# Attention stage of an RWKV and two-MLP kernel: new order of TensorE's work, six tiles in flight, and some work moved between VectorE, GpSimd and ScalarE

## The chip, the cores and the metric

The kernel runs on one core of one Trainium2 chip. The metric is the device time of one execution in microseconds (us). The core has five engines that run their own instruction queues in order: TensorE (PE in the profile; PEld is its weight load), VectorE (DVE), ScalarE (ACT), GpSimd (POOL) and SyncE (SP), which issues most transfers. They meet through semaphores.

## The reference

Three stages follow one another: an RWKV-like attention over 768 tokens of 4 sequences with 8 heads of 48, a mixture of 8 experts of which each token takes one, and a dense two-layer network.

```python
B, H, S, D = 4, 8, 768, 48
for t in range(S):                                   # attention
    cur = einsum('bhd,bhe->bhde', u[None] * k[:, :, t], v[:, :, t])
    y[:, :, t] = einsum('bhd,bhde->bhe', r[:, :, t], state + cur)
    state = w[None, :, :, None] * state + einsum('bhd,bhe->bhde', k[:, :, t], v[:, :, t])
x = y.transpose(0, 2, 1, 3).reshape(3072, 384)
logits = x @ w_gate                                  # (3072, 8)
e = argmax(logits, 1); gate = softmax(logits)[arange(3072), e]
x = gate[:, None] * (maximum(x @ w1[e], 0) @ w2[e])  # for each token its expert, 384 -> 1024 -> 384
h = x @ w_in                                         # 384 -> 2048
out = (h - tanh(h)) @ w_out                          # 2048 -> 384
```

## The kernel before

**Tiles.** The attention is cut into 6 chunks (`c`) of 128 tokens for each of the 4 sequences (`b`), which makes 24 tiles, `seq[n] = (n // 4, n % 4)`. One pass of the main loop, `for n in range(NN + 1)`, is called step n here. All of this is written in an order by hand (`tc.manual_schedule()`): each engine takes its instructions in the order in which the program issues them.

**One tile.** The token-by-token recurrence is done in matrix form. `load(n)` brings r, k, v by token (`n_b[n % NB]`) and r, k transposed (`t_b[n % NB]`). `scale` (line 312) multiplies the transposed r and k with tables of powers of the decay. `scores` (line 353) makes the 128 by 128 products of k and r for each head, in two PSUM banks, one for each half of the array's rows. `side_rk`, `side_rku`, `side_kh` (lines 317, 323, 332, GpSimd) make r*k, r*k*u and the scaled k; `diag_sum` (337, VectorE) sums r*k*u over a head, `diag` (344, ScalarE) puts the sum on the diagonal of a matrix `am` for each head. `mask` (359, VectorE) copies the scores of earlier keys from PSUM into `am`. `state` (370 to 377) adds the tile's k and v products to the running state `Sc[b]`: GpSimd multiplies the old state with the decay (`sw`, 376), VectorE adds the PSUM product (377). `state_copy` (385, ScalarE) puts the two 64-row halves of it into a block matrix `Sb[b]`. `outp` (393, 398) multiplies `Sb` with the scaled r over all 128 rows and `am` with v over 48 output columns, in turn for two pairs of heads, and ScalarE copies the result to `y` (403).

**Behind each chunk** of four tiles, spread over the next steps: `logits` and `logits2` (413 to 422, TensorE) and `gate` (428 to 449, VectorE: `m`, `sh`, `sc`, `mx`, `ssum`, `OH`, ...) choose an expert for every token; `rank_mm` (468 to 471, TensorE) and `rank_sel` (476 to 501) find its place in the expert's list: VectorE makes `pr`, the rank, `ge`, `hs`, `ohh`, `lo`; GpSimd makes from `ohh` the products `hv` (490) and a first `rh` (494), ScalarE or GpSimd the second `rh` (497, 499), VectorE `ol` (501); `idx_mm` (510, TensorE) adds up the list of token numbers. `xout` (524 to 533) transposes y back and writes it to DRAM. The gate runs in steps 6, 10, 14, 18, 22, the ranks one step later, the lists one step behind that.

**Weights.** Each float32 weight is split in two parts for TensorE's faster float32r form: `w_split` casts on ScalarE (`nc.scalar.copy`, line 84) and subtracts the cast from the original on an engine given as `eng` (line 85), in the attention stage VectorE by default, later mostly GpSimd. Steps 3 to 18 each do one quarter of a pair of weight blocks.

**The step before the change** issues, in this order: `load(n+3)`, on odd steps `w_load`; `diag_sum(n+1)`, `scale(n+1)`; `logits`; `outp(n-1)`, `state_copy(n-1)`; `xout`; `diag(n+1)`; `scores(n)`, `mask(n)`; `state(n)`; `side(n+2)`, `side_kh(n+2)`; `logits2`, `gate`; `rank_mm`, `rank_sel`; `idx_mm`; `w_split`. In step 1 GpSimd also makes the constants of the later stages (`consts`, `gate_cols`).

Behind the attention the experts' blocks and then the dense network follow, which the change doesn't touch.

Of the kernel before, what the change touches and what calls it, by code (L numbers as in the profile page):

```python
# [30 lines left out]
def rwkv_moe_moe_kernel(ctx: ExitStack, tc: tile.TileContext, rk_t, rkv, pk, u, wp1, wp2, out):  # L31
# [161 lines left out]
    NB = 5  # L193
# [8 lines left out]
    Sc = [ap_.tile([P, HP, D], F32, name=f"Sc{b}") for b in range(B)]  # L202
    Sb = [ap_.tile([P, HP, P], F32, name=f"Sb{b}") for b in range(B)]
# [3 lines left out]
    PRK = ap_.tile([P, 2, HP, P], F32, name="PRK")  # L207
# [5 lines left out]
    yh = [psy.tile([P, BANK], F32, tag=f"y{d}", name=f"yh{d}")[:, 0:HEAD] for d in range(KD)]  # L213
    Yp = [t.rearrange("p (j t) -> p j t", t=P) for t in yh[0:2]]
    Pb = yh[2]
    Pp = Pb[:, 0:HP * D].rearrange("p (j d) -> p j d", d=D)
# [52 lines left out]
    def tables():  # L269

        for t, base, n in ((pw, wsafe.unsqueeze(2), 16), (pq, pw[:, :, 16:17], 8)):
            nc.vector.memset(t[:, :, 0:1], 1.0)
            nc.vector.tensor_copy(out=t[:, :, 1:2], in_=base)
            m = 1
            while m < n:
                nc.vector.tensor_tensor(out=t[:, :, m + 1:2 * m + 1], in0=t[:, :, 1:m + 1],
                                        in1=bc(t[:, :, m:m + 1], [P, HP, m]), op=ALU.mult)
                m *= 2
        table(nc.gpsimd, PRK[:, 0], pq[:, :, 0:8], pw[:, :, 0:16])
# [3 lines left out]
        table(nc.vector, PRK[:, 1], ipq[:, :, 0:8], ipw[:, :, 1:17])  # L283
# [19 lines left out]
    def zero_states():  # L303
        for b in range(B):
            nc.scalar.mul(out=Sb[b], in_=ident.unsqueeze(1).to_broadcast([P, HP, P]), mul=0.0)
# [57 lines left out]
    def state(n):  # L363
        c, b = seq[n]
        if c == C - 1:
            return
        kh = st.pop(("kh", n))
        for j in range(HP):
            for q in range(2):
                nc.tensor.matmul(Pp[64 * q:64 * q + D, j, :], lhsT=kh[:, 2 * j + q, :],  # L370
                                 rhs=n_b[n % NB][:, 2, 2 * j + q, :], start=True, stop=True)
        if c == 0:
            nc.vector.tensor_copy(out=Sc[b], in_=Pp)
        else:
            sw = at2.tile([P, HP, D], F32, tag="sw", name="sw")
            nc.gpsimd.tensor_tensor(out=sw, in0=Sc[b], in1=bc(pq[:, :, 8:9], [P, HP, D]), op=ALU.mult)
            nc.vector.tensor_tensor(out=Sc[b], in0=sw, in1=Pp, op=ALU.add)
        st["S", b] = n

    def state_copy(n):  # L380
        c, b = seq[n]
        if c == C - 1:
            return
        for q in range(2):
            nc.scalar.copy(out=Sb[b][64 * q:64 * q + 64, :, 64 * q:64 * q + D], in_=Sc[b][64 * q:64 * q + 64, :, :])

    def outp(n):
        c, b = seq[n]
        am = st.pop(("am", n))
        for j0 in range(0, HP, 2):  # L390
            for j in (j0, j0 + 1):
                if c > 0:
                    nc.tensor.matmul(Yp[j % 2][:, j // 2, :], lhsT=Sb[b][:, j, :], rhs=t_b[n % NB][:, 0, j, :],
                                     start=True, stop=False)
            for j in (j0, j0 + 1):
                for q in range(2):
                    p0 = 64 * q
# [75 lines left out]
    def rank_sel(c):  # L473
# [16 lines left out]
        nc.gpsimd.tensor_tensor(out=hv.rearrange("p b (e q) -> p b e q", q=4),  # L490
# [3 lines left out]
        nc.gpsimd.tensor_tensor(out=rh[:, :, 0, :], in0=hv,  # L494
                                in1=bc(tileid[:, c * B:(c + 1) * B].unsqueeze(2), [P, B, E * 4]), op=ALU.mult)
        if c == C - 2:
            nc.gpsimd.tensor_scalar(out=rh[:, :, 1, :], in0=hv, scalar1=pid, scalar2=None, op0=ALU.mult)
        else:
            nc.scalar.activation(out=rh[:, :, 1, :], in_=hv, func=ACTF.Copy, scale=pid)
# [48 lines left out]
    xgh = [n_b[i][:, 0].rearrange("p h d -> p (h d)") for i in (4, 0)]  # L548
# [7 lines left out]
    def head_tiles():  # L556
        flat = [ap_.tile([P, 2 * HP * P], F32R, tag=f"t{i}", name=f"f{i}") for i in range(NB)]
        xth.extend(flat[i][:, 0:KD * HEAD].rearrange("p (k t) -> p k t", k=KD) for i in (4, 0))
        h2h.extend(flat[i][:, 0:2 * HEAD].rearrange("p (s t) -> p s t", s=2) for i in (1, 2, 3))
# [12 lines left out]
    xg0 = [n_b[i][:, 0].rearrange("p h d -> p (h d)") for i in (1, 2)]  # L572
# [36 lines left out]
    def by_token():  # L609

        with tc.tile_pool(name="slow", bufs=1) as sp:
# [3 lines left out]
            for b in range(B):  # L615
                nc.vector.memset(Sc[b], 0.0)
# [5 lines left out]
            for c in range(C):  # L622
                st["y", c] = yp.tile([P, HP, B, P], F32, tag="y", name="y")
                for b in range(B):
# [5 lines left out]
                    with tc.For_i(0, P, 1) as t:  # L630
                        nc.vector.tensor_copy(out=oh, in_=bc(ident[:, bass.ds(t, 1)], [P, 64]))
                        vb = ps1.tile([P, HP, P], F32, tag="X", name="vb", bufs=2)[:, :, 0:D]
                        for q in range(2):
                            nc.tensor.matmul(vb[64 * q:64 * q + 64], lhsT=oh,
                                             rhs=n_b[n % 2][:, 2].rearrange("p (j q) d -> p q j d", q=2)[:, q],
                                             start=True, stop=True)
                        nc.vector.tensor_tensor(out=kv, in0=vb, in1=bc(kT[:, :, bass.ds(t, 1)], [P, HP, D]), op=ALU.mult)
                        nc.vector.tensor_tensor(out=cur, in0=kv, in1=bc(ucol.unsqueeze(2), [P, HP, D]), op=ALU.mult)
                        nc.vector.tensor_add(out=cur, in0=cur, in1=Sc[b])
# [7 lines left out]
                        nc.vector.tensor_tensor(out=Sc[b], in0=Sc[b], in1=bc(wcol.unsqueeze(2), [P, HP, D]), op=ALU.mult)  # L647
                        nc.vector.tensor_add(out=Sc[b], in0=Sc[b], in1=kv)
# [12 lines left out]
    with tc.manual_schedule():  # L661
# [35 lines left out]
        for t in Yp + [Pp]:  # L697
            nc.vector.memset(t, 0.0)
# [3 lines left out]
        for n in range(NN + 1):  # L702
            if n + 3 < NN:
                load(n + 3)
            if n % 2 == 1 and n // 4 < PRE:
                w_load(n // 4, n // 2 % 2)
            if n + 1 < NN:
                diag_sum(n + 1)
                scale(n + 1)
            at_step(n, 2, logits)  # L710
            if 1 <= n <= NN:
                outp(n - 1)
                if n > 1:
                    state_copy(n - 1)
            for m in XOUT.get(n, (n - LAG,)):
                if m >= 0:
                    xout(m)
            if 0 < n < NN - 1:
                diag(n + 1)
            if n < NN:  # L720
# [5 lines left out]
                else:  # L726
                    if n == 1:
                        state(0)
                    state(n)
            if n == 1:  # L730
                state_copy(0)
            if n + 2 < NN:
                side(n + 2)
                if n == 0:
                    side_kh(0)
                    side_kh(1)
                side_kh(n + 2)
            at_step(n, 3, logits2)
            at_step(n, 3, gate)
            if n == H0 * B + 3:  # L740
                head_count()
            at_step(n, 4, rank_mm)
            at_step(n, 4, rank_sel)
            if n == H0 * B + 3:
                head_end()
            if n < NN:
                at_step(n, 5, idx_mm)
# [11 lines left out]
            if n >= 3 and (n - 3) // 4 < PRE:  # L759
                w_split((n - 3) // 4, (n - 3) % 4)  # L760
# [642 lines left out]
```

## Time and profile before

| | |
|---|---|
| median of 3 runs | 816.72 us (815.63 to 817.61) |
| the profiled execution | 815.03 us, of which the span of its instructions is 812.9 us |
| TensorE, VectorE, ScalarE, GpSimd busy over the span | 96%, 80%, 65%, 55% |
| mean granted clock of TensorE | 0.991 of full speed |
| scores of tile 0, 6, 22, 23 start at | 10.49, 44.22, 139.13, 144.60 us |

A row of the timeline reads: start (us), duration (us), engine, line of the kernel, operation, output <- inputs by the program's names, shapes, count, and in brackets the idle time of the engine just before and what ended it. Rows of the same kind that follow one another are merged with their count. A row of the groups by line has: line, engine, operation, names, shapes, count, then busy us and the mean ns of one, then the idle us before and what ended most of it. TensorE's rows overlap, since its instructions are pipelined: what a group costs is read from the start of the next. A GpSimd or VectorE row's duration can hold waiting.

### The profile page before, as it was taken

What the parts mean: (1) busy time and instruction counts of PE and PEld (TensorE: products, weight loads), DVE (VectorE), ACT (ScalarE), POOL (GpSimd) and SP (SyncE); (2) the same over time, 40 slices, a digit from 0 to 9 for tenths busy, and PEclk for the clock granted to TensorE, in tenths of its full rate; (3) what the DMA queues carried; (4) which work ended last, traced back from release to release, by engine and by line L of the source; (5) the groups of instructions that cost most, each with busy time, mean ns of one, the idle gap of its engine ahead of it and who ended that gap; (6) DMA issues with size and microseconds to landing.
All of it is one profiled execution on the core that took longest, in us unless ns stands there. A gap on an engine that the chain in (4) does not pass through costs nothing.

```text
span 812.9 us, 14403 instructions
## 1 busy us (share of the span) xinstructions
PE 780.9 (96%) x5052; PEld 699.3 (86%) x5052; DVE 648.6 (80%) x1127; ACT 526.0 (65%) x1135; POOL 450.7 (55%) x438
## 2 busy tenths in 40 slices
PE   7789999899999999999999999999999999999995
PEld 6567776699899999999989999999999999999895
DVE  7798988449888888995498888888888888888991
ACT  8778887426454545545587776776777677677770
POOL 7987885127676776775445544434345354343532
PEclk9999999999999999999999999999999999999998
DMA  8979864236689889995400000001000000000000
GB/s 220 268 205 260 219 200 135 89 92 188 199 223 267 268 207 276 321 240 160 136 1 0 1 10 30 2 0 40 1 1 30 10 1 20 21 1 10 30 1 39
DMA packets 34979, 89.88 MB, mean 111 GB/s; under 512 B 5690, under 2 KB 13022, under 8 KB 34896
## 3 DMA queue, kind: packets, MB, share of 16 engines
q1 hardware_dynamic: 30704, 78.87, 34.2%
q0 software_dynamic: 4192, 9.99, 4.1%
q8 instruction: 42, 0.69, 0.4%
q14 instruction: 41, 0.34, 0.2%
HBM read 73.10 MB, written 15.74 MB: 109 GB/s over the span
## 4 chain that ended last, share of the span: by engine, by line
PE 49%; DVE 2%; issue 1%; POOL 1%; ACT 0%; POOLq 0%; DVEq 0%; ACTq 0%
PE h L1239 24%; PE o L1287 22%; PE y L1013 2%; PE hps L988 1%; DVE t L1260 0%; DVE h L1257 0%; DVE h L1258 0%; DVE h L1256 0%; DVE t L1255 0%; POOL out_dram L1300 0%; POOL g L1276 0%; ACT g L1275 0%; POOLq L1398 0%; ACT z L1243 0%; ACT t L1245 0%
## 5 line engine op out<-in xcount | busy, mean ns | idle before, releaser
L1276 POOL TENSOR_TENSOR g<-t,g 128x512 fp32r<-128x512 f32 x93 | 120.4, 1295 | 176.3 <-ACT g L1275 122.6
L1239 PE MATMUL h<-xb,ring 128*128 128x512 f32 x864 | 215.9, 395 | 0.7 <-DVE t L1260 0.7
L1287 PE MATMUL o<-ring,g 128*128 128x384 f32 x1116 | 209.3, 336 | 0.0
L1287 PEld LDWEIGHTS o<-ring,g 128*128 128x128 f32 x1116 | 196.1, 188 | 8.1
L1239 PEld LDWEIGHTS h<-xb,ring 128*128 128x128 f32 x864 | 161.3, 188 | 31.9 <-DVE t L1260 1.1
L85 POOL TENSOR_TENSOR ring<-stg,ring 128x384 fp32r<-128x384 f32 x102 | 105.0, 1052 | 57.1 <-ACT ring L84 50.2
L1243 ACT ACTIVATE z<-h 128x512 f32<-128x512 f32 x96 | 57.5, 599 | 98.0 <-PE h L1239 97.9
L1013 PE MATMUL y<-h,ring 128*128 128x256 f32 (+7 forms) x576 | 113.9, 342 | 0.0
L988 PE MATMUL hps<-xt,ring 128*128 128x472 f32 (+6 forms) x504 | 106.1, 354 | 1.8 <-DVE xt L977 0.9
L1013 PEld LDWEIGHTS y<-h,ring 128*128 128x128 f32 x576 | 101.4, 188 | 3.2
L1255 DVE TENSOR_TENSOR t<-t,h 128x512 f32<-128x512 f32 x96 | 65.7, 684 | 41.8 <-ACT t L1245 41.3
L988 PEld LDWEIGHTS hps<-xt,ring 128*128 128x128 f32 x504 | 90.5, 188 | 6.0 <-DVE xt L977 1.6
L84 ACT CAST ring<-stg 128x384 fp32r<-128x384 f32 x152 | 70.8, 512 | 19.1 <-DMA stg<-in_wp_dram 18.6
L1260 DVE COPY_PREDICATED t<-mk,h 128x512 f32<-128x512 uint32 x96 | 72.1, 751 | 9.9
L1257 DVE SCALAR_TENSOR_TENSOR h<-s,h 128x512 f32<-128x512 f32 x96 | 66.9, 696 | 11.4 <-ACT g L1275 1.4
L991 ACT ACTIVATE h<-hps 128x256 fp32r<-128x256 f32 (+7 forms) x64 | 32.0, 501 | 58.2 <-PE hps L988 50.7
L1247 ACT ACTIVATE s<-z,gb 128x512 f32<-128x512 f32 x96 | 69.6, 725 | 0.0
L1258 DVE SCALAR_TENSOR_TENSOR h<-z,h 128x512 f32<-128x512 f32 x96 | 66.8, 696 | 3.3
L1249 ACT ACTIVATE mk<-z,gt 128x512 f32<-128x512 f32 x96 | 69.3, 722 | 0.0
L1256 DVE TENSOR_TENSOR h<-h,z 128x512 f32<-128x512 f32 x96 | 66.4, 692 | 0.0
L1275 ACT CAST g<-t 128x512 fp32r<-128x512 f32 x93 | 57.6, 619 | 7.9 <-DVE t L1260 5.7
L344 ACT ACTIVATE am<-ident,dt 128x128 f32<-128x128 f32 x192 | 58.6, 390 | 4.4 <-DVE dt L337 4.2
(233 smaller groups left out, 1112.9 us busy)
## 6 DMA issues: line engine op xcount, KB each, us to landing
stg<-in_wp_dram SPq DMA_DIRECT2D x64, 384.0 KB
n<-in_rkv_dram SPq DMA_DIRECT2D x24, 576.0 KB
d<-in_wp_dram SPq DMA_DIRECT2D x32, 384.0 KB
t<-in_rk_t_dram SPq DMA_DIRECT2D x48, 192.0 KB
wdec<-dcf SPq DMA_DIRECT2D x32, 192.0 KB
xd<-xs SPq DMA_DIRECT2D x24, 192.0 KB
stg<-wdec SPq DMA_DIRECT2D x12, 384.0 KB
wl<-wdec SPq DMA_DIRECT2D x2, 768.0 KB
```

Source lines behind the costliest of these rows:

```text
L84: nc.scalar.copy(out=dst[:, 0, sl], in_=of)
L85: eng.tensor_tensor(out=dst[:, 1, sl], in0=of, in1=dst[:, 0, sl].bitcast(F32), op=ALU.subtract)
L988: nc.tensor.matmul(ps, lhsT=wf(a, kk), rhs=xt[e][b][:, kk, :], start=(n == 0), stop=(n == 8))
L1013: nc.tensor.matmul(yps[d], lhsT=wf(a)[:, d * P:(d + 1) * P], rhs=h2[:, b, :], start=(f == 0 and n == 0), stop=(f == CH1 - 1 and n == 2))
L1239: nc.tensor.matmul(ps, lhsT=wf(a, kk), rhs=xb[j][:, b, kk, :], start=(n == 0), stop=(n == 8))
L1247: nc.scalar.activation(out=s, in_=z, func=ACTF.Square, scale=G_K ** 0.5, bias=gb)
L1249: nc.scalar.activation(out=mk, in_=z, func=ACTF.Relu, scale=-1.0, bias=gt2)
L1257: nc.vector.scalar_tensor_tensor(out=ps, in0=s, scalar=G_K * G_D, in1=ps, op0=ALU.add, op1=ALU.mult)
L1258: nc.vector.scalar_tensor_tensor(out=ps, in0=z, scalar=G_A, in1=ps, op0=ALU.subtract, op1=ALU.mult)
L1260: nc.vector.copy_predicated(out=t, mask=mk.bitcast(U32), data=ps)
L1276: nc.gpsimd.tensor_tensor(out=g[:, 1, :], in0=ww, in1=g[:, 0, :].bitcast(F32), op=ALU.subtract)
L1287: nc.tensor.matmul(ops[q], lhsT=gg[i][:, b, q * P:(q + 1) * P], rhs=wf(a), start=(f == 0 and n == 0), stop=(f == CH2 - 1 and n == 2))
```

## The change

- The step is issued in a new order: `y_copy(n-2)` (the copy of y, now one instruction over all heads), `diag_sum(n+1)`, `diag(n+1)`, `scores(n)`, `mask(n)`, `scale(n+1)`, `xout`, `logits2`, `rank_mm`, `idx_mm` (one step later than before), `logits`, `state(n)`, `outp(n-1)`, `side(n+2)`, `gate`, `rank_sel`, `w_split`.
- `outp` first does all products with the state, each on 64 rows by 48 columns for one head and straight from `Sc`, then all products with v, into one bank. `Sb`, `state_copy` and `zero_states` go; `Sc` is kept twice, for even and odd chunks.
- Six tile buffers instead of five, and loads one tile further ahead.
- `scale` becomes two VectorE instructions; the table of powers for r lies in a PSUM bank and is made on VectorE instead of GpSimd.
- In `rank_sel`, `hv` and both `rh` are made on VectorE.
- `w_split` of steps 3 to 18 subtracts on GpSimd.
- `consts` and `gate_cols` move from step 1 to the start of the program.

```diff
-    NB = 5
+    NB = 6
-    Sb = [ap_.tile([P, HP, P], F32, name=f"Sb{b}") for b in range(B)]
+    Sc = [[ap_.tile([P, HP, D], F32, name=f"Sc{b}{i}") for i in range(2)] for b in range(B)]
-    PRK = ap_.tile([P, 2, HP, P], F32, name="PRK")
+    PK = ap_.tile([P, HP, P], F32, name="PK")
+    yb = [psy.tile([P, BANK], F32, tag=f"y{d}", name=f"yh{d}") for d in range(KD)]
+    Yp, PR = (t.rearrange("p (j t) -> p j t", t=P) for t in yb[0:2])
...
     def scale(n):
         t = t_b[n % NB]
-        nc.vector.tensor_tensor(out=t, in0=t, in1=PRK, op=ALU.mult)
+        for i, pw_ in enumerate((PR, PK)):
+            nc.vector.tensor_tensor(out=t[:, i], in0=t[:, i], in1=pw_, op=ALU.mult)
...
+        if c > 0:
+            for j in range(HP):
                 for q in range(2):
                     p0 = 64 * q
+                    nc.tensor.matmul(Yp[p0:p0 + D, j, :], lhsT=Sc[b][(c - 1) % 2][p0:p0 + 64, j, :],
+                                     rhs=t_b[n % NB][p0:p0 + 64, 0, j, :], start=(j == 0), stop=False)
+        for j in range(HP):
+            for q in range(2):
+                p0 = 64 * q
+                nc.tensor.matmul(Yp[p0:p0 + D, j, :], lhsT=n_b[n % NB][:, 2, 2 * j + q, :],
+                                 rhs=am[:, q, j, :], start=(c == 0 and j == 0), stop=(j == HP - 1))
+    def y_copy(n):
...
+        nc.scalar.copy(out=st["y", c][:, :, b, :], in_=Yp)
...
-        nc.gpsimd.tensor_tensor(out=hv.rearrange("p b (e q) -> p b e q", q=4),
+        nc.vector.tensor_tensor(out=hv.rearrange("p b (e q) -> p b e q", q=4),
...
-        nc.gpsimd.tensor_tensor(out=rh[:, :, 0, :], in0=hv,
+        nc.vector.tensor_tensor(out=rh[:, :, 0, :], in0=hv,
...
-            nc.scalar.activation(out=rh[:, :, 1, :], in_=hv, func=ACTF.Copy, scale=pid)
+        nc.vector.tensor_scalar(out=rh[:, :, 1, :], in0=hv, scalar1=pid, scalar2=None, op0=ALU.mult)
...
         for n in range(NN + 1):
-            if n + 3 < NN:
-                load(n + 3)
+            for m in (3, 4) if n == 0 else (n + 4,):
+                if m < NN:
+                    load(m)
...
-                w_split((n - 3) // 4, (n - 3) % 4)
+                w_split((n - 3) // 4, (n - 3) % 4, eng=nc.gpsimd)
```

## Rows read from the trace of the kernel before

**Rows 1.** Timeline of TensorE: scores of tile 6 and of tile 22.

```profile
44.22 1.16 PE L353 MATMUL A<-t 64*128 64x128 f32 x16
...
139.13 1.16 PE L353 MATMUL A<-t 64*128 64x128 f32 x16
```

**Rows 2.** Stretches: length, busy us of each engine, clock, DMA share, GB/s.

```profile
20.00:30.00 10.00, 6.24 (x92) 5.11 (x90) 5.44 (x10) 6.85 (x23) 9.72 (x32) 0.85 1.03 279
44.20:139.10 94.90, 89.11 (x1083) 67.03 (x1081) 84.63 (x171) 75.69 (x232) 74.47 (x72) 0.98 0.73 205
```

**Rows 3.** Timeline of TensorE in step 18, up to step 19.

```profile
116.51 1.16 PE L353 MATMUL A<-t 64*128 64x128 f32 x16
117.60 0.56 PE L370 MATMUL yh<-n,kh 128*48 128x48 f32 x16
118.09 1.06 PE L422 MATMUL sm<-sel,lt 128*128 128x8 f32 x8
119.01 0.69 PE L393 MATMUL yh<-t,Sb 128*128 128x128 f32 x4
...
122.00 1.16 PE L353 MATMUL A<-t 64*128 64x128 f32 x16
```

**Rows 4.** Groups by line, 44.2 to 139.1 us.

```profile
L312 DVE TENSOR_TENSOR t<-t,PRK 128x1024 f32<-128x1024 f32 x17 | 25.7, 1514 | 0.0
L359 DVE COPY_PREDICATED am<-mlt,A 128x512 f32<-128x512 uint32 x32 | 21.4, 722 | 1.9 <-PE A L353 1.9
...
L85 DVE TENSOR_TENSOR ring<-stg,ring 128x384 fp32r<-128x384 f32 x13 | 9.5, 728 | 6.6 <-ACT ring L84 6.5
...
L84 ACT CAST ring<-stg 128x384 fp32r<-128x384 f32 x13 | 6.5, 497 | 0.0
```

**Rows 5.** Timeline of GpSimd, steps 14 and 15.

```profile
94.91 0.52 POOL L376 TENSOR_TENSOR sw<-Sc,pq 128x192 f32<-128x192 f32 x1
...
96.45 1.00 POOL L323 TENSOR_TENSOR rku<-rk,ub 128x384 f32<-128x384 f32 x1
97.41 1.00 POOL L332 TENSOR_TENSOR kh<-n,KT 128x384 f32<-128x384 f32 x1
103.57 0.92 POOL L490 TENSOR_TENSOR hv<-OH,ohh 128x128 f16<-128x128 f16 x1 [5.16 <-DVE lo L488]
```

**Rows 6.** Timeline of ScalarE and VectorE: a diagonal, gate and ranks.

```profile
45.38 2.45 ACT L344 ACTIVATE am<-ident,dt 128x128 f32<-128x128 f32 x8
...
96.67 0.83 DVE L443 TENSOR_TENSOR OH<-sc,mx 128x32 f16<-128x32 f32 x1
97.42 1.02 DVE L444 TENSOR_SCALAR ssum<-ssum 128x4 f32<-128x4 f32 x1
...
102.40 0.18 DVE L476 TENSOR_TENSOR pr<-sm,OH 128x32 f32<-128x32 f32 x1
...
103.54 0.69 DVE L501 TENSOR_TENSOR ol<-iotaf,lo 128x512 f16<-128x512 f32 x1
...
142.62 0.16 DVE L444 TENSOR_SCALAR ssum<-ssum 128x4 f32<-128x4 f32 x1
```

**Rows 7.** Lines 377 and 1255 (ns minimum, median, maximum); line 85 on GpSimd.

```profile
L377 DVE TENSOR_TENSOR Sc<-sw,yh x16: 323/334/345, 37.5 to 125.7; 128x192 f32<-128x192 f32 x16
...
L1255 DVE TENSOR_TENSOR t<-t,h x96: 661/686/691, 404.8 to 791.1; 128x512 f32<-128x512 f32 x96
...
L85 POOL TENSOR_TENSOR ring<-stg,ring 128x384 fp32r<-128x384 f32 x102 | 105.0, 1052 | 57.1 <-ACT ring L84 50.2
```

**Rows 8.** Timeline of GpSimd and TensorE in the first steps.

```profile
6.54 1.00 POOL L317 TENSOR_TENSOR rk<-n 128x384 f32<-128x384 f32 x1 [2.63 <-DMA n<-in_rkv_dram]
...
24.85 0.22 POOL L145 MEMSET ones<- 128x128 f16 x1
...
27.73 0.21 POOL L250 COPY wgp<-pkt 128x32 f32<-128x32 f32 x1
...
26.79 2.45 PE L398 MATMUL yh<-am,n 128*48 128x128 f32 x16 [2.07 <-ACT am L344]
```

More of the change, by code (lines that the diff above doesn't have):

```diff
@@ L212, in rwkv_moe_moe_kernel @@
     KT = ap_.tile([P, H, D], F32, name="KT")
[L213 to L216, printed above, removed]
+    yb = [psy.tile([P, BANK], F32, tag=f"y{d}", name=f"yh{d}") for d in range(KD)]
+    yh = [t[:, 0:HEAD] for t in yb]
+    Yp, PR = (t.rearrange("p (j t) -> p j t", t=P) for t in yb[0:2])
+    Pp = yb[2][:, 0:HP * D].rearrange("p (j d) -> p j d", d=D)
     headn = ap_.tile([P, 1], F32, name="headn")
@@ L278, in tables @@
                 m *= 2
-        table(nc.gpsimd, PRK[:, 0], pq[:, :, 0:8], pw[:, :, 0:16])
+        table(nc.vector, PR, pq[:, :, 0:8], pw[:, :, 0:16])
         nc.vector.reciprocal(out=ipw, in_=pw)
@@ L282, in tables @@
         nc.vector.tensor_tensor(out=ipl, in0=ipq, in1=bc(pq[:, :, 8:9], [P, HP, 9]), op=ALU.mult)
[L283 removed]
+        table(nc.vector, PK, ipq[:, :, 0:8], ipw[:, :, 1:17])
     def table(eng, dst, fa, fb):
@@ L371, in state @@
                                  rhs=n_b[n % NB][:, 2, 2 * j + q, :], start=True, stop=True)
+        new = Sc[b][c % 2]
         if c == 0:
-            nc.vector.tensor_copy(out=Sc[b], in_=Pp)
+            nc.vector.tensor_copy(out=new, in_=Pp)
         else:
             sw = at2.tile([P, HP, D], F32, tag="sw", name="sw")
[L376 to L385, printed above, removed]
+            nc.gpsimd.tensor_tensor(out=sw, in0=Sc[b][(c - 1) % 2], in1=bc(pq[:, :, 8:9], [P, HP, D]), op=ALU.mult)
+            nc.vector.tensor_tensor(out=new, in0=sw, in1=Pp, op=ALU.add)
     def outp(n):
@@ L547, in rwkv_moe_moe_kernel @@
     xth, h2h = [], []
-    xgh = [n_b[i][:, 0].rearrange("p h d -> p (h d)") for i in (4, 0)]
+    xgh = [n_b[i][:, 0].rearrange("p h d -> p (h d)") for i in (1, 2)]
     hps = []
@@ L696, in rwkv_moe_moe_kernel @@
         side(1)
-        for t in Yp + [Pp]:
+        for t in (Yp, Pp):
             nc.vector.memset(t, 0.0)
@@ L702, in rwkv_moe_moe_kernel @@
         for n in range(NN + 1):
-            if n + 3 < NN:
-                load(n + 3)
+            for m in (3, 4) if n == 0 else (n + 4,):
+                if m < NN:
+                    load(m)
             if n % 2 == 1 and n // 4 < PRE:
                 w_load(n // 4, n // 2 % 2)
+            if n >= 2:
+                y_copy(n - 2)
             if n + 1 < NN:
                 diag_sum(n + 1)
[L709 to L719, printed above, removed]
+                if n > 0:
+                    diag(n + 1)
             if n < NN:
@@ L725, in rwkv_moe_moe_kernel @@
                     diag(1)
[L726 to L734, printed above, removed]
                     side_kh(0)
                     side_kh(1)
-                side_kh(n + 2)
+            if n + 1 < NN:
+                scale(n + 1)
+            for m in XOUT.get(n, (n - LAG,)):
+                if m >= 0:
+                    xout(m)
             at_step(n, 3, logits2)
-            at_step(n, 3, gate)
             if n == H0 * B + 3:
@@ L742, in rwkv_moe_moe_kernel @@
             at_step(n, 4, rank_mm)
+            if n < NN:
+                at_step(n, 6, idx_mm)
+            at_step(n, 2, logits)
+            if 0 < n < NN:
+                if n == 1:
+                    state(0)
+                state(n)
+            if n > 0:
+                outp(n - 1)
+            if n == NN:
+                y_copy(NN - 1)
+            if n + 2 < NN:
+                side(n + 2)
+                side_kh(n + 2)
+            at_step(n, 3, gate)
             at_step(n, 4, rank_sel)
```

40 lines of the change are left out of this document (10 added, 30 removed).

## Prediction, made before the change was run

> **What bounds the kernel now.** I read the busy shares by stretch first, for the attention stage alone: its 24 tiles (steps n = 0 to 23) fill the first fifth of the span, and the change touches nothing behind it. Between the scores of tiles 6 and 22, which start at 44.22 and 139.13 us [rows 1], 16 tiles take 94.91 us: 5.93 us a tile, 23.73 us a group of four. In that stretch TensorE is booked 89.1 us, VectorE 84.6, ScalarE 75.7, GpSimd 74.5 [rows 2]: no engine has much room, so I looked for who waits.
>
> TensorE's order in time shows its work without a stall. In step 18 it runs back to back from 116.51 to 122.00 us: scores 1.09 us, state 0.49, logits2 0.92, then `outp` and the transposes of `xout` together 2.99 [rows 3]. Without logits2 a step is 4.57 us of TensorE. So of 5.93 us more than a microsecond is not TensorE's own work.
>
> The groups by line give VectorE's account in the same stretch: `scale` 1.51 us a tile, `mask` two times 0.72, and the first weight splits 0.73 each, ahead of whose 13 VectorE also sat idle for 6.5 us in all, until ScalarE's cast of 0.50 was done [rows 4]. With `diag_sum`, the state update and the gate and rank chains it is busy or held by that cast for 91 of the 94.9 us (84.6 + 6.5) [rows 2, 4]. VectorE's queue sets the pace; TensorE and ScalarE fit around it.
>
> The reader should then see how GpSimd and VectorE hold each other. `ssum`, four elements, takes 1.02 us from 97.42 to 98.44 while GpSimd's `kh` runs from 97.41 to 98.41; the one before it, `OH`, took 0.83 us and ended as `rku` ended (97.45). With GpSimd idle the same `ssum` takes 0.16 us [rows 5, 6]. A VectorE instruction of this kind waits for the GpSimd instruction in flight, and two in a row wait for two. By contrast the state update, one operand in PSUM, takes 323 to 345 ns all 16 times [rows 7]: it is never held. And the rank chain is never held before the change, because GpSimd is standing at its own `hv`, waiting 5.16 us for VectorE's `lo` [rows 5]: from `pr` at 102.40 to the end of `ol` at 104.23 it takes 1.83 us [rows 6].
>
> The Trainium skill, page "SBUF — State Buffer", section "Who interferes with whom", says the same: a VectorE instruction with two SBUF inputs and a GpSimd instruction that reads SBUF exclude each other, and the second fully blocks. The trace agrees by the 1.02 us above.
>
> **The change, part by part**, per group of four tiles in steps 6 to 17, where every step carries a split.
>
> (a) Splits to GpSimd. VectorE loses 0.73 + 0.50 us a tile: -4.9 us a group. GpSimd gains 1.05 us a tile by the same subtraction later in this kernel [rows 7]; its queue is then `sw` 0.52, `rk`, `rku`, `kh` about 1.0 each [rows 5] and 1.05, about 4.6 us: under the step, so not the bound. But the split stands in order behind ScalarE's cast, and the cast behind `diag`, 2.45 us for its eight [rows 6]. What is queued behind the split is all of GpSimd's next step.
>
> (b) `scale` in two halves, the table of R in PSUM. A 512-element VectorE multiply with an operand in PSUM is 0.69 us [rows 7]; the 512-element `ol`, both inputs in SBUF, is 0.69 as well [rows 6]. Two are 1.38 against 1.51, which held some waiting already. The R half should not be held; the K half can be, by nothing up to one GpSimd instruction of 1.0; I take 0.3, since GpSimd stands waiting for the cast in about half the steps. +0.7 a group (-0.5 to +3.5).
>
> (c) Three rank products to VectorE. Their work alone: bounded by `pr`, 0.18, and `ol`, 0.69 [rows 6]; nearer `pr`, 0.25 each: +0.75 a group. The fourth wait, of GpSimd on `lo`, goes.
>
> (d) With that wait gone, GpSimd works through the rank chain. In a step VectorE now does `diag_sum`, `mask`, `scale`, state update, then rank: the chain starts some 3.2 us after `diag_sum` (0.54 + 1.3 + 1.4, less overlaps). `diag_sum` also releases `diag` on ScalarE (2.45 us), then a tile copy and the cast follow, about half a microsecond each as the cast's 0.50 [rows 4]: the split starts at about 3.8 us, with 4.6 us of GpSimd work behind it. `ohh`, `lo`, `hv` and both `rh` have two SBUF inputs or the form of `ssum` and stand one after the other: each waits for one GpSimd instruction, as `OH` and `ssum` did. Bounds: nothing, and five times 1.0. The order in time puts it near the upper one; since `sw` is only 0.5 and the first may slip through, I take +3.3 a group.
>
> (e) The gate loses the same cover in part: GpSimd no longer pauses after it. Bounds 0 and twice the 0.86 that `ssum` lost; +0.7.
>
> (f) TensorE grouped by shape, `outp` last. A step without logits2 falls from 4.57: one pair of switches inside `outp` goes, and the 64-row state products cost about what the 64-row scores do (16 instructions, 1.09 us) against 8 full-array ones. Roughly 4.2 us. It buys little, as TensorE isn't what the group waits for: `outp` no longer waits for the mask, but the scores of n+1 now wait for `scale(n+1)`, which VectorE does after `mask(n)`, one step ahead instead of two. So behind the rank chain stand `diag_sum`, `mask` and `scale` (3 us) before TensorE can go on, and in the step with the logits VectorE waits for the scores instead. From walking four steps I put VectorE's wait for scores at 1.8 us a group, where 1.9 us in the whole stretch stood before [rows 4]: +1.3.
>
> Sum: -4.9 + 0.7 + 0.75 + 3.3 + 0.7 + 1.3 = +1.85 us a group; three groups +5.5. Steps 18 to 21 have one split to lose (a: -1.2); without splits GpSimd is partly idle in the rank chain (b 0.3, d 1.5, e 0.3), and steps 20 and 21 have no state (f 0.4); c stays 0.75: +2.
>
> (g) Constants moved to the start. Now they hold GpSimd from 24.85 to 27.94 us; TensorE then waits 2.07 us and runs the next 16 products in 2.45 us instead of about 1.14 [rows 8], with the granted clock at 0.85 of full speed over 20 to 30 us [rows 2], that is partly at 1.2 GHz instead of 2.4. At the start GpSimd waits 2.63 us for the first tile [rows 8], which hides most of the 3.1. Gain 2.07 + 1.3, and some of the early steps' slack: -3.7 (0 to -4.5). If the cover is gone, the 0.5 us left over lands ahead of tile 0.
>
> (h) Hidden or nil: the block copies of the state leave ScalarE, which isn't the bound; the merged copy of y; zeroing for a sixth tile replaces that of the states at the start; the load one tile earlier has its data in time already (no wait on a load after tile 2). The tail behind step 23 keeps its instructions: 0, within 1 us.
>
> Total +5.5 + 2 - 3.7 = +3.8 us. The profiled execution took 815.03 us (span 812.9), so 818.8; the median of the runs is 816.72, 1.7 above, and on that scale the forecast is **820.5 us**.
>
> The Trainium skill, page "Perfetto Trace Analysis", section "Optimizing Scalar/DVE Operations", speaks against the split's move: work offloaded between these two engines may not help, as they share a read port. By (a) alone the stage would gain 16 us; by (d) and (e) most of it comes back.
>
> **Rivals.** *The waits stay small* (chance 0.32). If VectorE's short instructions find gaps, as the rank chain did at 102.40 [rows 6], (d) is 0 to 1.7 and (e) 0: a group is -2.2 to -0.5, with (g) the total is -10 to -4: 807 to 813 on the scale of the median. For it: two of the chain's seven may fall into GpSimd's wait for the cast. Against: `OH` and `ssum` [rows 6]. It decides when the rank chain in a step with a split is under 3.8 us.
>
> *They cancel* (0.16): (d) about 2.2 and (e) about 0.4, total within 0.2%, 815.1 to 818.3. 0.2% (1.6 us) is about what a measurement of this kernel can tell from no change.
>
> *The state products run one at a time* (0.08). Both halves now write one bank (partitions 0 to 47 and 64 to 111), where the scores' halves write two. If they don't overlap, 16 instructions cost 2.1 us instead of 1.09, and a step of TensorE 5.2: about +1 in the two steps of a group that TensorE bounds, +8 in all: 828. For it: no row shows two row halves into one bank; against: the state's own 48-column products into two partition halves of one bank take 0.49 us for 16 [rows 3]. The Trainium skill, page "TensorEngine Tiling (Array Packing)", "Gotcha 1: PSUM Pressure", says that different row tiles can't access one bank at a time; no row of before shows that.
>
> *The change does nothing, as its parts lie off the path*: excluded for (a), VectorE being booked or held 96% of the stretch.
>
> **How the numbers follow.** Likeliest (0.44): the collision as summed, 820.5, its own range 818.4 to 825: the upper end is (d) at 4.5 and a clock that falls in TensorE's wait of 3 to 4 us behind each rank chain, as it did in (g), at some 1 us each. Slower 0.44 + 0.08 = 0.52, same 0.16, faster 0.32. The range runs from the middle of the small-waits case, 809, to 829, the case of one bank.
>
> **What would show it.** Right: `ohh`, `lo`, `hv`, `rh` in steps 7, 11 and 15 take up to 1 us each and end with GpSimd's instructions; the rank chain is 5 us or more; TensorE then waits on `scale`; tile 6's scores start near 40.5 us; 16 tiles from there take some 102 us. Wrong: a rank chain under 3 us, a group under 23 us, or `outp`'s first 16 instructions near 2 us.

## The result, and the profile after

The changed kernel takes 824.48 us (median of 4 runs, 821.82 to 826.78) against 817.16 us for the kernel before on the same chip (4 runs, 815.63 to 819.22): ratio 1.0082, 95% interval 1.0061 to 1.0104. It is slower by about 0.8%. Its profiled execution took 821.82 us, 6.8 more than that of before, with a span of 820.0.

Where the time lies is read from TensorE's timeline, at the scores of tiles 6 and 22, as in [rows 1]. Profile after (start, duration in us):

```profile
42.04 1.16 PE L351 MATMUL A<-t 64*128 64x128 f32 x16
...
144.23 1.16 PE L351 MATMUL A<-t 64*128 64x128 f32 x16
...
156.06 0.87 PE L556 MATMUL hp<-ident,n 128*128 128x128 f32 x6
```

The last row is the first transposes of the head, the next stage; before, they stand here:

```profile
148.97 0.88 PE L564 MATMUL hp<-ident,n 128*128 128x128 f32 x6
```

Tile 6 comes 2.2 us earlier than in [rows 1]. The 16 tiles behind it take 102.19 us instead of 94.91, 7.3 more: 3.7 in the first three groups of four (75.94 against 72.29) and 3.6 in the last (26.25 against 22.62). From the scores of tile 22 to the first transposes of the head 11.8 us pass instead of 9.8, 2.0 more. Together that is +7.1 us; what lies behind is 0.3 shorter, which gives the 6.8.

The busy shares of the same stretch and of the early steps, to be held against [rows 2] (length; busy us of TensorE, its weight loads, VectorE, ScalarE, GpSimd; granted clock; DMA share; GB/s):

```profile
42.00:144.20 102.20, 84.20 (x1212) 68.55 (x1209) 83.61 (x185) 62.91 (x181) 73.40 (x78) 0.90 0.70 197
20.00:30.00 10.00, 5.89 (x87) 5.21 (x89) 6.57 (x12) 5.21 (x17) 7.99 (x8) 0.83 1.02 274
```

TensorE and ScalarE have less to do than before and the stage is longer: time went into waits. VectorE and GpSimd are booked about as long as before, although 13 splits changed sides. The clock fell from 0.98 to 0.90.

The groups by line of this stretch, beside [rows 4]: the halves of `scale`, `mask` with its wait for scores, the scores, and the split on GpSimd.

```profile
L351 PE MATMUL A<-t 64*128 64x128 f32 x256 | 22.6, 319 | 18.0 <-issue 17.4 <-PE yh L391 0.7
L357 DVE COPY_PREDICATED am<-mlt,A 128x512 f32<-128x512 uint32 x32 | 21.4, 722 | 13.5 <-PE A L351 13.5
L85 POOL TENSOR_TENSOR ring<-stg,ring 128x384 fp32r<-128x384 f32 x14 | 14.0, 1002 | 18.5 <-ACT ring L84 12.5 <-DVE OH L438 4.0 <-DVE ssum L439 1.9
L310 DVE TENSOR_TENSOR t<-t,PK 128x512 f32<-128x512 f32 x16 | 13.6, 850 | 0.0
L310 DVE TENSOR_TENSOR t<-t,yh 128x512 f32<-128x512 f32 x16 | 10.7, 670 | 0.0
```

VectorE waits 13.5 us for scores, where it waited 1.9 [rows 4]; TensorE waits 17.4 us ahead of scores; GpSimd stands 18.5 us ahead of its splits.

The rank chain of step 11, VectorE's timeline, and the GpSimd instructions that run meanwhile. In [rows 6] such a chain (step 15), from `pr` to the end of `ol`, took 1.83 us.

```profile
76.33 0.18 DVE L471 TENSOR_TENSOR pr<-sm,OH 128x32 f32<-128x32 f32 x1
...
77.28 0.74 DVE L480 TENSOR_TENSOR ohh<-hs,q 128x16 f16<-128x16 f32 x1
77.94 0.15 DVE L483 SCALAR_TENSOR_TENSOR lo<-hs,RK 128x4 f32<-128x4 f32 x1
78.06 0.57 DVE L485 TENSOR_TENSOR hv<-OH,ohh 128x128 f16<-128x128 f16 x1
78.66 0.97 DVE L489 TENSOR_TENSOR rh<-hv,tileid 128x128 f16<-128x128 f16 x1
79.55 1.06 DVE L491 TENSOR_SCALAR rh<-hv,pid 128x128 f16<-128x128 f16 x1
80.53 1.53 DVE L493 TENSOR_TENSOR ol<-iotaf,lo 128x512 f16<-128x512 f32 x1
```

```profile
76.99 1.00 POOL L85 TENSOR_TENSOR ring<-stg,ring 128x384 fp32r<-128x384 f32 x1
77.95 0.53 POOL L375 TENSOR_TENSOR sw<-Sc,pq 128x192 f32<-128x192 f32 x1
78.44 1.04 POOL L315 TENSOR_TENSOR rk<-n 128x384 f32<-128x384 f32 x1
79.56 1.00 POOL L321 TENSOR_TENSOR rku<-rk,ub 128x384 f32<-128x384 f32 x1
80.52 0.99 POOL L330 TENSOR_TENSOR kh<-n,KT 128x384 f32<-128x384 f32 x1
85.94 1.00 POOL L85 TENSOR_TENSOR ring<-stg,ring 128x384 fp32r<-128x384 f32 x1 [4.43 <-ACT ring L84]
```

Four VectorE instructions end at most 0.15 us behind the end of a GpSimd instruction: `ohh` at 78.02 behind the split (77.99), `hv` at 78.63 behind `sw` (78.48), the two `rh` at 79.63 and 80.61 behind `rk` (79.48) and `rku` (80.56); `lo` passes between the first two unheld, in 0.15 us, and `ol` needs 0.55 us more than `kh` (82.06 and 81.51). The chain takes 5.73 us; in steps 7, 15 and 19 it takes 4.92, 5.72 and 4.50. Then GpSimd stands for 4.43 us: it had done its work at VectorE's cost and waits for a cast that hangs on VectorE's `diag_sum`.

TensorE meanwhile has no scaled tile:

```profile
79.52 1.08 PE L391 MATMUL yh<-am,n 128*48 128x128 f32 x16
85.02 2.17 PE L351 MATMUL A<-t 64*128 64x128 f32 x16 [4.43 <-issue]
87.12 1.11 PE L516 MATMUL Xps<-ident,y 128*128 128x128 f32 x4
```

The scores behind the stand take 2.17 us instead of 1.16, at half the full clock (1.2 instead of 2.4 GHz); the granted clock over 80 to 90 us is 0.70. The same happens behind the chains of steps 7 and 19 (2.07, 2.17) and 15 (2.07).

### The profile page after: what moved, and what is told of

The parts are those of the page before. It is cut to its first block, busy times and chain, and to the rows that moved or that the text cites. A ratio compares the mean times of both kernels' runs of the same rounds, so it can differ in the third digit from the quotient of the medians.

```text
span 820.0 us, 14700 instructions
## 1 busy us (share of the span) xinstructions
PE 773.8 (94%) x5212; PEld 700.9 (85%) x5212; DVE 645.5 (79%) x1153; ACT 509.3 (62%) x1064; POOL 443.6 (54%) x440
## 2 busy tenths in 40 slices
DMA packets 34981, 89.92 MB, mean 110 GB/s; under 512 B 5690, under 2 KB 13022, under 8 KB 34896
## 4 chain that ended last, share of the span: by engine, by line
PE 48%; DVE 2%; issue 1%; POOL 1%; ACT 0%; POOLq 0%; DVEq 0%; ACTq 0%
PE h L1232 23%; PE o L1280 22%; PE y L1006 2%; PE hps L981 1%; DVE t L1253 0%; DVE h L1250 0%; DVE h L1251 0%; DVE h L1249 0%; DVE t L1248 0%; POOL out_dram L1293 0%; POOL g L1269 0%; ACT g L1268 0%; POOLq L1391 0%; ACT z L1236 0%; ACT t L1238 0%
## 5 line engine op out<-in xcount | busy, mean ns | idle before, releaser
L85 POOL TENSOR_TENSOR ring<-stg,ring 128x384 fp32r<-128x384 f32 x118 | 121.2, 1045 | 77.5 <-ACT ring L84 58.0
```

The costliest lines, as they stand in the source:

```text
L85: eng.tensor_tensor(out=dst[:, 1, sl], in0=of, in1=dst[:, 0, sl].bitcast(F32), op=ALU.subtract)
```

## Experiments

Ratios are to the kernel before, run on the same chip between the runs of each kernel. Two theories stood at the start. *Collision*: the rank products' move makes VectorE and GpSimd block each other in the rank chain. *Order*: the new order is what costs, above all that scores wait for `scale` behind `mask`.

**1. Undo and do alone: the products, the splits.** The edit of `a_rank_back`, in the changed kernel:

```
-        nc.vector.tensor_tensor(out=hv.rearrange("p b (e q) -> p b e q", q=4),
+        nc.gpsimd.tensor_tensor(out=hv.rearrange("p b (e q) -> p b e q", q=4),
...
-        nc.vector.tensor_tensor(out=rh[:, :, 0, :], in0=hv,
+        nc.gpsimd.tensor_tensor(out=rh[:, :, 0, :], in0=hv,
...
-        nc.vector.tensor_scalar(out=rh[:, :, 1, :], in0=hv, scalar1=pid, scalar2=None, op0=ALU.mult)
+            nc.scalar.activation(out=rh[:, :, 1, :], in_=hv, func=ACTF.Copy, scale=pid)
```

`a_both_back` also takes the split back; `b_split` and `b_split_rank` make the same edits forwards in the kernel before:

```
-                w_split((n - 3) // 4, (n - 3) % 4, eng=nc.gpsimd)
+                w_split((n - 3) // 4, (n - 3) % 4)
```

> The changed kernel with the three rank products back where they were (hv and a first rh on GpSimd, the second rh on ScalarE or GpSimd); all else as changed. Collision theory (the rank chain waits for GpSimd's instructions, one for one): GpSimd stands at hv again, the chain in steps 7, 11, 15 falls from 4.9 to 5.7 us to about 2.0, TensorE's stall two steps later from 3.6 to 5 us to under 1.5, and its clock stays up: 3 us and 1 to 2 us of clock in each of four groups, 808 to 813 us. Order theory (the loss is the new order: scale(n+1) behind mask(n), one tile ahead): only the products' own 0.75 us a group, about 821 us.

Measured 810.49 us, 0.9924 (0.9907 to 0.9940): 13 to 14 us less than the changed kernel. The chains take 2.04 to 2.05 us and the 16 tiles 90.96. Collision hit, order missed. Scores of tiles 6 and 22:

```profile
43.63 1.16 PE L351 MATMUL A<-t 64*128 64x128 f32 x16
...
134.59 1.16 PE L351 MATMUL A<-t 64*128 64x128 f32 x16
```

> The changed kernel with the rank products and also the splits' subtractions back where they were: the new order, six tiles, the halves of scale and the early constants alone. Collision theory: the chain is about 2 us, but VectorE pays 1.2 us in each step for the split again: a group near the 23.7 us of before, 815 to 819 us. Order theory: VectorE's extra 4.9 us a group comes on top of the changed kernel's pace, 835 us or more.

Measured 809.68 us, 0.9924 (0.9901 to 0.9947); 16 tiles 89.92. Both theories missed: the rest of the change, without the two moves, is worth -0.8%, and the splits on GpSimd are worth nothing beside it. Scores of tiles 6 and 22:

```profile
42.62 1.16 PE L351 MATMUL A<-t 64*128 64x128 f32 x16
...
132.54 1.16 PE L351 MATMUL A<-t 64*128 64x128 f32 x16
```

> The kernel before with one edit: the splits of steps 3 to 18 subtract on GpSimd. Collision theory: GpSimd still stands at hv during the rank chain, so the chain stays at 1.8 to 2 us; VectorE loses 4.9 us a group and TensorE's own 21 us a group is next: 2 to 2.8 us a group less, 806 to 810 us. Order theory: the same; the run is the base for the next one.

Measured 816.73 us, 1.0004 (0.9992 to 1.0016). A miss: 16 us of splits and waits for casts left VectorE and no time was gained. The waits say why. VectorE's own waits in the stretch of 16 tiles of `b_split` (engine, line, waited for: us in all, times, longest):

```profile
DVE dt L337 <- POOL rku L323: 8.9, 7, 1.7
DVE am L359 <- PE A L353: 5.1, 5, 1.4
```

Before, it waited 6.5 us for casts, 1.9 for scores [rows 4] and not at all for `rku`. GpSimd, for its part, had stood 16.6 us at its four `hv` before (5.16 of them in [rows 5]) and stands 0.7 there now: it is booked 88.83 of 94.80 us and has little room left. As it no longer stands there, VectorE's rank chains are held too, up to 3.02 us (2.55, 2.05, 3.00, 3.02), where 1.8 to 2 were expected. GpSimd's splits, all 14 of them in the trace (ns minimum, median, maximum), are held in turn by VectorE, as the one at 107.12 us, which starts with a `scale` of VectorE (107.14, 1.21 us) and takes 2.10:

```profile
L85 POOL TENSOR_TENSOR ring<-stg,ring x14: 997/1987/2097, 47.8 to 123.5; 128x384 fp32r<-128x384 f32 x14
```

The stretch as a whole:

```profile
47.10:141.90 94.80, 88.54 (x1083) 66.95 (x1081) 79.82 (x158) 75.00 (x232) 88.83 (x86) 0.98 0.72 205
```

> The kernel before with both moves (splits to GpSimd, rank products to VectorE) and the old order. Collision theory: the chain grows to 4.5 to 6 us in the old order too and takes back 3 us a group of what the splits gave: 815 to 822 us. Order theory: no more than the products' own 0.75 us a group above the run with the splits alone, 809 to 813 us.

Measured 822.56 us, 1.0079 (1.0051 to 1.0106): 5.8 us above `b_split`, with chains of 4.65 to 5.41 us, and just above what the collision theory gave; the order theory missed. The collision costs in the old order too, less than half as much.

**2. The collision against the products' own work.** In the changed kernel GpSimd is made to stand during the chain, and the products stay on VectorE:

```
         st["ol", c], st["rh", c] = ol, rh
+        pz = gp.tile([P, 1], F16, tag="pz", name="pz")
+        nc.gpsimd.tensor_copy(out=pz, in_=ol[:, B - 1, P - 1:P])
```

> The changed kernel with one addition: behind the rank chain's last VectorE instruction a one-column GpSimd copy reads its result, so that GpSimd stands during the chain, as it did before the change, while the three rank products stay on VectorE. Collision theory (VectorE's short instructions wait for GpSimd's): the chain falls from 4.5 to 5.7 us to about 3 (2.05 as with the products back, and three products of about 0.3), and the time to 811 to 816 us. Rival (what costs is that VectorE does the products at all): the chain stays above 4 us and the time at 822 to 827.

Measured 813.17 us, 0.9946 (0.9930 to 0.9963). Collision hit. GpSimd and VectorE of this kernel in step 11:

```profile
79.88 0.19 POOL L497 COPY pz<-ol 128x1 f16<-128x1 f16 x1 [3.24 <-DVE ol L493]
80.02 1.01 POOL L85 TENSOR_TENSOR ring<-stg,ring 128x384 fp32r<-128x384 f32 x1
```

```profile
77.38 0.18 DVE L471 TENSOR_TENSOR pr<-sm,OH 128x32 f32<-128x32 f32 x1
...
78.23 0.17 DVE L480 TENSOR_TENSOR ohh<-hs,q 128x16 f16<-128x16 f32 x1
78.32 0.15 DVE L483 SCALAR_TENSOR_TENSOR lo<-hs,RK 128x4 f32<-128x4 f32 x1
78.44 0.29 DVE L485 TENSOR_TENSOR hv<-OH,ohh 128x128 f16<-128x128 f16 x1
78.76 0.29 DVE L489 TENSOR_TENSOR rh<-hv,tileid 128x128 f16<-128x128 f16 x1
78.97 0.25 DVE L491 TENSOR_SCALAR rh<-hv,pid 128x128 f16<-128x128 f16 x1
79.13 0.69 DVE L493 TENSOR_TENSOR ol<-iotaf,lo 128x512 f16<-128x512 f32 x1
```

The chain takes 2.44 us (79.82 less 77.38), 0.4 more than with the products elsewhere. The same instructions that took 0.57, 0.97, 1.06 and 1.53 us take 0.29, 0.29, 0.25 and 0.69 with GpSimd standing. An engine that is made to wait 3.24 us makes the kernel 11 us faster.

**3. The half clock behind the stand.** Dummy products in the changed kernel keep TensorE at work:

```
+            if n in (9, 13, 17, 21):
+                keep_warm(16)
             if n < NN:
                 scores(n)
```

> The changed kernel with 16 dummy TensorE products of 128x128 ahead of the scores of tiles 9, 13, 17 and 21, where TensorE stands for 3.6 to 5 us. If the half clock behind that stall is a cost of its own, those scores fall from 2.1 to about 1.2 us, VectorE's wait for them goes with it, and the time is 818 to 822 us. If the clock's fall is covered by other waits: 823 to 826, and the groups of four tiles stay at 24.7 to 26.3 us.

Measured 817.53 us, 1.0008 (0.9992 to 1.0025): 6 to 7 us less than the changed kernel, the better end of what was expected. The chains are as long as there (5.45, 5.73, 5.71, 4.50) and TensorE works on nothing of use, but the scores of tile 13 now run in 1.25 us (the row of the dummies counts each twice):

```profile
80.74 3.84 PE L535 MATMUL warm<-ident 128*128 128x128 f32 x32
85.26 1.25 PE L351 MATMUL A<-t 64*128 64x128 f32 x16 [0.68 <-PE warm L535]
86.44 0.66 PE L516 MATMUL Xps<-ident,y 128*128 128x128 f32 x4
87.21 1.07 PE L408 MATMUL lps<-y,wgp 128*32 128x512 f32 x8
```

The 16 tiles take 97.99 us, 4.2 less:

```profile
41.95 1.16 PE L351 MATMUL A<-t 64*128 64x128 f32 x16
...
139.94 1.16 PE L351 MATMUL A<-t 64*128 64x128 f32 x16
```

So of the 11.2 us between the changed kernel and `a_rank_back` in this stretch (102.19 to 90.96), 4.2 are the clock's and 7.0 the collision's itself. In the profiled execution the rest of the gain, 1.7 us, lies behind tile 22, where the two kernels are the same; no run shows why.

**4. The order within VectorE.** `scale(n + 1)` moves ahead of `mask(n)`, in the changed kernel (`a_first`) and in `a_both_back` (`c_first`):

```
                 scores(n)
+                if n + 1 < NN:
+                    scale(n + 1)
                 mask(n)
...
-            if n + 1 < NN:
-                scale(n + 1)
```

> The changed kernel with one thing exchanged: in each step VectorE scales tile n+1 before it masks tile n, not after. Order theory (term f): behind each rank chain the scores then start some 1.3 us earlier, and VectorE masks while TensorE computes them; groups of four tiles shrink by 1.3 us or more from 24.7 to 26.3, and the time is 814 to 819 us. Rival (VectorE's queue is full, so the order in it is worth nothing): 822 to 826.

Measured 818.47 us, 1.0040 (1.0022 to 1.0057): the time that the order theory gave, but not by its way. The 16 tiles take 102.26 us, as long as in the changed kernel; the gain is ahead of them (1.0 us) and behind them (2.3 us of the profiled execution); what makes it there was not followed up. The scores of tile 13 show what took the wait's place:

```profile
85.07 1.87 PE L351 MATMUL A<-t 64*128 64x128 f32 x16 [3.13 <-DVE am L357]
```

Scores are written to one pair of buffers, and now wait for `mask(12)` to have read them (first half from 84.30 us on): the start is 85.07 instead of 85.02.

> The same exchange in the version with rank products and splits back where they were (809.7 us). If the scores' wait for the scale costs there too: VectorE's waits for the scores (0.87 to 3.1 us each) go, and the time is 803 to 807. If VectorE's own 22 us a group set the pace: 808 to 811.

Measured 810.40 us, 0.9948 (0.9929 to 0.9968). No gain: the order of the two is worth nothing there.

**5. Two parts by themselves.** `b_consts` is the kernel before with `consts()` and `gate_cols()` moved from step 1 to behind `later_keys()`; `c_mixed` is `a_both_back` with `outp` in fours:

```
+        for j0 in range(0, HP, 2):
+            for j in (j0, j0 + 1):
+                for q in range(2):
...
+                        nc.tensor.matmul(Yp[p0:p0 + D, j, :], lhsT=Sc[b][(c - 1) % 2][p0:p0 + 64, j, :],
...
+            for j in (j0, j0 + 1):
+                for q in range(2):
...
+                    nc.tensor.matmul(Yp[p0:p0 + D, j, :], lhsT=n_b[n % NB][:, 2, 2 * j + q, :],
```

> The kernel before with one part of the change: the constants written by GpSimd at the start and not in step 1. Forecast (term g): TensorE's wait of 2.07 us and the half clock behind it go, 812 to 814 us, scores of tile 6 some 3.7 us earlier than at 44.22. Rival (other waits of the first steps take the place): 815.5 to 818.5.

Measured 814.42 us, 0.9982 (0.9969 to 0.9995): -1.5 us, between the two ranges. The scores of tile 6 start at 43.92 instead of 44.22 [rows 1], and the wait that was to go is still there, beside [rows 8]:

```profile
27.25 2.46 PE L398 MATMUL yh<-am,n 128*48 128x128 f32 x16 [2.07 <-ACT am L344]
```

GpSimd no longer writes constants, but its `rk` at 16.44 has waited 1.80 us for a tile's load, and `dt`, behind which ScalarE's diagonal waits, follows GpSimd's `rku` at 24.42.

> The changed kernel with rank products and splits back where they were (809.7 us), and in it the two kinds of y products by turns in fours (four 64-row ones, then four 128-row ones, and so on), as the kernel before did with its own. If the grouping by shape is where this version's gain of 6 us over the kernel before comes from, each tile's y products grow by about 0.5 us and the time comes back to 814 to 819 us. If the gain comes from the order and the scale in halves, TensorE's time being covered: 809 to 811.

Measured 813.31 us, 0.9945 (0.9924 to 0.9966): between the two, and its interval overlaps that of `a_both_back`. The y products take 2.29 us a tile in fours and 2.02 grouped; the 16 tiles are 2.1 us longer, all of it in the first four; the other three groups take the same to 0.03 us. `c_best` below has the code of `a_both_back` in these steps, and its 16 tiles take 91.36 us, 1.4 more, also in the first four: so much two traces can differ by themselves. Grouping is worth some 2 us at most, not the whole 6.

**6. Half the splits; dummies elsewhere.** `c_half` is `a_rank_back` with the split on GpSimd in odd steps only; `c_best` is `a_both_back` with `keep_warm(14)` between the states of tiles 0 and 1 and `keep_warm(18)` behind the last index products.

> The changed kernel with the rank products back on GpSimd and ScalarE, and the weight splits by turns on GpSimd (odd steps) and VectorE (even steps). If with all splits on GpSimd that engine sets the pace and with all on VectorE that one does, half and half loosens both: 804 to 808 us, groups of 20.5 to 21.5 us. If TensorE or the loads set the pace of both: 809 to 811, groups of 21.7 to 22.5.

Measured 812.29 us, 0.9941 (0.9924 to 0.9958). A miss: groups of 22.5, 22.5, 22.2 and 25.2 us, no shorter than with all splits on one engine. In its 16 tiles neither engine is full (VectorE 79.79, GpSimd 71.87 of 92.30 us), but VectorE waits 5.9 us for scores and TensorE 7.6 us ahead of scores, which start as soon as `scale` has ended: each waits for the other.

> The version with rank products and splits back where they were, and dummy TensorE products of 128x128 in two places where its trace shows a stand of 2.9 to 3.5 us and half clock behind it: 14 between the state products of tiles 0 and 1 (half clock from 22.4 to about 26 us), and 18 behind the last index products, ahead of the first expert's y products (half clock from 157.6 to 163 us). If the half clock behind a stand costs time wherever TensorE then has work waiting: 1.4 us less in the second place and up to 1.9 in the first, together 806 to 808.5 us, ratio to the kernel before 0.988 to 0.991. If other waits cover it: 809 to 811, ratio 0.992 to 0.994.

Measured 810.41 us, 0.9943 (0.9921 to 0.9964). A miss. In the first place the scores of tile 2 run at full clock, but start at 26.44 us instead of 24.91: the dummies run until 25.15, and in `a_both_back` the stand ended at 22.39. In the second, too, the dummies outlast the stand that they were to fill (3.5 us in `a_both_back`, from 154.0 to 157.57): the y products start 5.7 us behind the first dummy, 1.4 of it in a wait for TensorE's own sequencer (PEq).

```profile
156.15 4.26 PE L538 MATMUL warm<-ident 128*128 128x128 f32 x36
161.85 0.17 PE L800 MATMUL sm<-cum,ones 128*128 128x8 f16 x1 [1.44 <-PEq L790]
161.88 1.31 PE L596 MATMUL yh<-f,ring 128*128 128x256 f32 x9
```

Of the versions that beat both kernels `a_both_back` and `a_rank_back` (0.9924 each) are the fastest; their intervals part them neither from each other nor from the other five (0.9941 to 0.9948).

## Why the prediction was right, and where it was not

Slower by the collision in the rank chain, 820.5 us: the sign and the mechanism are right, and `a_pause` shows the mechanism at work. The sum for the 16 tiles (forecast +7.5, measured +7.3) is right by luck, since two large errors cancel in it:

| 16 tiles from tile 6, us | forecast | measured |
|---|---|---|
| products to VectorE: (c), (d) | +14.4 | +11.2 (changed kernel less `a_rank_back`) |
| splits to GpSimd: (a) | -15.9 | +1.0 (`a_rank_back` less `a_both_back`) |
| the rest there: (b), (e), (f) | +9.1 | -5.0 (`a_both_back` less the kernel before) |

(The forecasts add up to 7.6, which was rounded.) `c_best` has the code of `a_both_back` in these steps; with its 91.36 us the last two rows are -0.4 and -3.5, which changes nothing in the reading. Nor does the time lie where it was put: 5.5 us were forecast for the first three groups and 2 for the last, and 3.7 and 3.6 were measured.

*What bounds the kernel* failed in what was drawn from it. VectorE is busy or waits for casts and scores for 93.0 of 94.9 us before (84.6 + 6.5 + 1.9), so its queue may well have set the pace; but "TensorE and ScalarE fit around it" made it the only limit. `b_split` frees VectorE of 16 us and the time stays, since others stand right behind it. GpSimd is full there. TensorE's own work in the old order is 21.9 us a group (in `b_split` a group of 22.66 us, 71.98 to 94.64, has 0.8 us of waits), so of 23.7 us no more than 1.9 could go. In `c_half`, with the new order, neither VectorE nor GpSimd is full, and it is no faster either.

*(a)* was mis-sized: forecast -4.9 us a group, measured -0.6 (`b_split`) and -0.4 or -0.9 (`a_rank_back` against `a_both_back` or `c_best`) in steps 6 to 17. Some 2 us are lost again in the group behind them, so that the 16 tiles gain nothing in either order. GpSimd's queue was put at 4.6 us a step and called free; with `hv` and `rh`, and with splits of 1.99 us in the median in `b_split`, where 1.05 were taken from later in the kernel, it is 22.2 us a group (88.83 / 4). The prediction let GpSimd hold VectorE, and not VectorE GpSimd.

*(b)* The R half is never held (0.67 us), as forecast; the K half takes 0.85. Together 24.3 us for 16 tiles, as much as the 1.51 us each before [rows 4]: 0 instead of +0.7 a group.

*(c), (d)* The chain grew as forecast: 4.05 us longer in steps 7, 11 and 15 and 2.25 in step 19 were forecast, 2.9, 3.7, 3.9 and 2.7 measured. (c) alone is 0.4 (`a_pause`) instead of 0.75. But the sum charged each us of the chain to the group, and 13.1 us of longer chains cost 7.0. The clock that the prediction named for its upper end came at each of the four chains, 1.05 us each (4.2 / 4, `a_warm`), and should have stood in the sum.

*(e)* had the wrong sign. The gate, from `m` to the end of `cum`, takes 2.64, 2.17, 2.17 and 2.17 us instead of 3.43, 2.59, 3.46 and 2.97, 0.8 less a group. In steps 10, 14 and 18 GpSimd stands about 2 us ahead of its split during the gate, as ScalarE's cast stands behind the gate's `ex` (in step 10 `ex` starts at 71.37, the cast ends at 71.99 and the split starts at 72.08; the groups of after name `OH` and `ssum`, which end at nearly the same time).

*(f)* In the changed kernel VectorE's wait for scores is 3.4 us a group (13.5 / 4), where 1.8 were forecast. But the new order without the two moves is a gain, 16 tiles in 89.92 us against 94.91. "It buys little, as TensorE isn't what the group waits for" overlooked how close TensorE stood; in `a_both_back` it is booked 77.15 us, 12 less than before [rows 2]:

```profile
42.60:132.50 89.90, 77.15 (x1211) 63.32 (x1209) 79.81 (x187) 64.46 (x186) 63.21 (x67) 1.00 0.76 217
```

That the gain comes from these 12 us is not shown: `c_mixed` puts 1.1 us a group back on TensorE and loses nothing in three groups of four. Most of it can be found in VectorE's rows: four instructions of the gate (`sc`, `OH`, `ssum`, `cum`) take 4.8 us in the stretch instead of 8.7, and VectorE waits 6.6 us for casts and scores instead of 8.4. GpSimd stands 21.7 us at `hv` there, 16.6 before. This is an account and not an experiment.

*(g)* was forecast at -3.7 and is -1.5 us alone (`b_consts`). The wait of [rows 8] was put down to the constants on GpSimd in the same window, and it stays when they go. The trace of before showed it: the diagonal that TensorE waits for stands behind a `dt` that waited for `rku`, and `rku` ended at 23.96 us, before the constants begin at 24.85.

```profile
23.99 0.55 DVE L337 TENSOR_REDUCE dt<-rku 128x8 f32<-128x384 f32 x1 [1.34 <-POOL rku L323]
...
24.64 2.45 ACT L344 ACTIVATE am<-ident,dt 128x128 f32<-128x128 f32 x8 [0.30 <-DVE dt L337]
```

*(h)* The tail was put at 0 within 1 us and costs 2.0 in the changed kernel, 1.5 in `a_both_back`: with `outp` last, the y products of tiles 22 and 23 both stand behind the last scores, and those of tile 23 wait 0.69 us for the copy of tile 22. This, and the 1.5 us that tile 6 gained less than forecast, make most of the 4 us between forecast and result.

```profile
154.04 1.08 PE L386 MATMUL yh<-t,Sc 64*48 64x128 f32 x16 [0.69 <-ACT y L398]
```

*The rivals.* The small waits did not come: the chains lie above the 3.8 us that decided. That the change does nothing was excluded for (a), as VectorE is booked or held 96% of the stretch; `b_split` shows that (a) alone does nothing. State products into one bank: 16 rows take 1.08 us and the next group starts 1.01 behind (74.27 and 75.28 us of the changed kernel), 0.06 us a row where the dummies of `a_warm`, which use all rows, take 0.12 (3.84 / 32), so the halves overlap. The Trainium skill's "TensorEngine Tiling (Array Packing)", "Gotcha 1: PSUM Pressure", which the prediction weighed, is not borne out for two row tiles that write different partitions of one bank.

*A reading.* The 1.02 us that the prediction gives as the trace's agreement with a rule for two inputs in SBUF are those of `ssum`, which adds a constant to one tensor (line 444); the row with two inputs is `OH`'s, 0.83 us. That both were held stands.

*What stays open.* With the products back, all splits on VectorE, on GpSimd, or half on each give the same time within the intervals. In each, waits for the other engines take the place of what is removed. The loop from `scale` over the scores and `mask` to the next `scale`, which has one pair of score buffers, may hold the period at 22 us a group; a second pair was not tried. Why the group behind the last splits takes 25.2 us in `a_rank_back` and `c_half` and 22.9 in `a_both_back` was not followed up. How the -6 us of the rest divide is known in part: constants 1.5, grouping up to 2.

## What to carry to other kernels

A wait on an idle engine can be the cover of another: before moving work off an engine that stands waiting, see who runs undisturbed meanwhile, and if it must be moved, keep the stand with a tiny instruction that reads the chain's last result. When one of two coupled engines looks full, remove its load alone before believing in the gain: where waits only change their cause, the next limit stands right behind. A sum that comes out is no proof of its terms: undo them one by one. A stand of TensorE costs twice where half clock follows it; dummy products fill it, if they end before the work that it waits for is ready.

## What the runs showed that was not expected

GpSimd is held by VectorE as VectorE is by GpSimd: the same split takes 1.00 us in the mean in the changed kernel and 1.99 in the median in `b_split`, where it falls together with the full-size `scale`. The Trainium skill's "SBUF — State Buffer", "Who interferes with whom", has the two exclude each other, which these rows bear out from GpSimd's side as well. And 64 dummy products that compute nothing, with no other edit, gave back 6 to 7 of the 7 us that the change had cost, 4.2 of them in the 16 tiles where they stand.
